# First expert step on idle accumulator banks, with its w1 sums on TensorE and the other sums of weights later

## The chip, the cores and the metric

The kernel runs on one core of one Trainium2 chip. The metric is the device time of one execution in microseconds. Of each kernel one execution was also profiled.

In the profile's lines PE is TensorE, PEld its weight loads, DVE is VectorE, ACT is ScalarE, POOL is GpSimd, SP is the queue that issues most loads. SBUF and PSUM are the memories on the chip; TensorE's results come into banks of PSUM. The granted clock is the share of TensorE's full clock that the trace gives: 1.00 (I call the array warm) or 0.50 (cold), with means between for a stretch that has both. A count such as "x4" counts records of the trace, and here one matmul leaves two of them.

## The reference, cut to what matters

```python
for c in range(nc):                        # Mamba-2 chunks, one after another
    cum = np.cumsum(np.log(a[chunk]))
    L = np.exp(cum_i - cum_j) * causal     # decays between positions
    y = ((C @ B.T) * L) @ x + (C @ state) * np.exp(cum)
    state = decay_full * state + sum(B x decay_from_j)
x = y.transpose(...)                       # 3072 tokens x 256
p = domain_probs / (domain_probs.sum(-1) + 1e-9)
for e in range(4):                         # four experts, 256 -> 1024 -> 256
    out += p[:, e] * (np.maximum(x @ w1[e], 0) @ w2[e])
```

The kernel handles a sequence in chunks of 128 positions and the experts in blocks of 512 tokens. There are six blocks of eight steps; a step is half of one expert. Each pair of matrix products in a step is done by a scheme of seven products in place of eight. The scheme needs sums of blocks of the weights (S1 to S4), sums of blocks of the tokens (yS) and sums of the seven results.

## The kernel before

The first block's four chunks have to pass before its first expert step can go beyond its first two products. These are the parts that matter. Names on the left of a `<-` in the profile are the tiles named here.

```python
def sums_of(op):                              # 4 GpSimd operations, then a store by GpSimd
    nc.gpsimd.tensor_add(op(S1), op(S3), op(A22))
    nc.gpsimd.tensor_sub(op(S2), op(S1), op(A11))
    nc.gpsimd.tensor_sub(op(S4), op(A12), op(S2))
    nc.gpsimd.tensor_sub(op(S3), op(A11), op(S3))

def decays(c):
    ...
    LT = att.tile([P, NH * P], FP32, tag="LT", name="LT", bufs=1)      # one buffer
    nc.vector.tensor_tensor_scan(out=LT, data0=s["ab"], data1=ident..., ...)
    ...
    nc.gpsimd.tensor_mul(bdec, xb..., s["LT"][:, :, P - 1:P]...)       # GpSimd reads LT
    ...
    nc.vector.tensor_tensor_scan(out=dec, data0=s["ah"], data1=zeros, ...)
    nc.gpsimd.tensor_mul(cts, s["ctm"], dec...)

for c in range(CPB):                          # the four chunks of the first block
    masks(c)                                  # ScalarE
    ...
    scores(c, acc_banks)                      # TensorE
    ...                                       # loads, gates (c == 0)
    if c == 2:
        opened(0)                             # products 1 and 2 of the first step
    decays(c)                                 # VectorE, GpSimd
    if c:
        carry(c - 1)                          # VectorE: S, M
    masked(c, range(NQ))                      # VectorE: MT
    added(c, ps_att, "att")                   # TensorE: A <- bdec
    outputs(c, ps_att, "att")                 # TensorE: y; ScalarE: yT
    if c == 1: load_chunk(4); sum_w1(0)       # GpSimd
    if c == 2: load_chunk(5); sum_w2(0)
total(0, 1, "11"); gated(0, "11", "z11"); sums(0); carry(CPB - 1)
sum_w1(1); sum_w2(1)

for n in range(NS + 1):                       # the steps, software-pipelined
    ...
    if c_in is not None:
        masks(c_in)
        decays(c_in)                          # a later chunk: LT, dec on VectorE
    ...
    smul(n - 1, 1); fmul(n, 6); snap(n, 6); smul(n - 1, 3)
    fmul(n, 5); fmul(n, 7); snap(n, 7)
    total(n, 7, "22")                         # VectorE: z from bank Y
    smul(n - 1, 7); smul(n - 1, 5)
    gated(n, "22", "z22")                     # VectorE: h
    ...
    fmul(n, 3)                                # into bank Y again: waits for that z
    ...
```

The order in each engine's queue is the program's order; the waits between engines are set by the tile framework.

## Time and profile before

| | before |
|---|---|
| median of the first three executions | 680.82 us (679.91 to 680.96) |
| the profiled execution | 678.77 us, span 677.0 us |
| TensorE busy | 643.3 us, 95% |
| VectorE busy | 504.7 us, 75% |
| GpSimd busy | 107.9 us, 75 of them before 120 us |

The shares of busy time hide two stages. From 53.5 us on TensorE works almost without a gap. Before that VectorE works through four chunks and one expert step, and TensorE mostly waits. The change is about that first stage alone. The page's slices of 17 us show it: in the rows below each character is a slice, and a digit the share of it that the engine was busy, in tenths.

```profile
PE   3779999999999999999999999999999999999995
PEld 1458788888888887888887888887888888888884
DVE  6979887697776867876878768668868776856655
```

### The profile page before, as it was taken

The numbers are of one execution on the slowest core, as the hardware profiler recorded it, in microseconds if no ns is written. First come the engines' busy times: TensorE is split into PE (matmuls) and PEld (weight loads), VectorE is DVE, ScalarE is ACT, GpSimd is POOL, SyncE is SP. The second block draws the span as 40 slices with busy tenths as digits, with TensorE's granted clock in tenths as the row PEclk, the third lists the DMA queues.
The fourth block names the chain that finished last, engine by engine and source line by source line (L and its number), as shares of the span: only waits on it lengthen the run. The fifth ranks groups of instructions, "written<-read, shape, count | busy, mean of one in ns | idle before, by whom it ended". The sixth has DMA issues, their size and how long they took to land.

```text
span 677.0 us, 9047 instructions
## 1 busy us (share of the span) xinstructions
PE 643.3 (95%) x3465; PEld 538.6 (80%) x3465; DVE 504.7 (75%) x821; ACT 116.2 (17%) x231; POOL 107.9 (16%) x153
## 2 busy tenths in 40 slices
PE   3779999999999999999999999999999999999995
PEld 1458788888888887888887888887888888888884
DVE  6979887697776867876878768668868776856655
ACT  1111112121211121121112111212211112111110
POOL 2976845001000002000002000002000000200000
PEclk9989999999999999999999999999999999999999
DMA  8997859636745554765364655554673543653202
GB/s 247 337 326 251 293 194 345 245 120 183 253 160 182 189 201 129 243 234 180 121 231 153 205 188 193 196 179 163 186 258 127 180 161 109 171 218 119 99 1 31
DMA packets 70938, 128.64 MB, mean 190 GB/s; under 512 B 29040, under 2 KB 52464, under 8 KB 70896
## 3 DMA queue, kind: packets, MB, share of 16 engines
q1 hardware_dynamic: 65688, 112.67, 49.3%
q0 software_dynamic: 2304, 14.68, 5.7%
q10 hardware_dynamic: 2904, 0.72, 0.5%
q8 instruction: 27, 0.44, 0.3%
q14 instruction: 15, 0.12, 0.1%
HBM read 109.99 MB, written 18.07 MB: 189 GB/s over the span
## 4 chain that ended last, share of the span: by engine, by line
PE 89%; DVE 6%; issue 0%; ACT 0%; POOL 0%; DMA 0%; DVEq 0%
PE acc L409 41%; PE X L365 24%; PE Y L365 19%; DVE h L387 2%; PE y L310 2%; PE g L271 2%; PE y L303 1%; DVE hT L394 1%; DVE LT L237 1%; DVE z L377 0%; DVE u L429 0%; PE A L292 0%; ACT snap L372 0%; DVE MT L281 0%; DVE ot L445 0%
## 5 line engine op out<-in xcount | busy, mean ns | idle before, releaser
L377 DVE TENSOR_TENSOR z<-Y,snap 128x512 f32<-128x512 f32 x144 | 99.0, 688 | 131.6 <-ACT snap L372 109.3
L409 PE MATMUL acc<-hT,wt 128*128 128x256 f32 x768 | 191.2, 382 | 0.0
L372 ACT COPY snap<-X 128x512 f32<-128x512 f32 x144 | 84.3, 585 | 487.8 <-PE X L365 481.5
L409 PEld LDWEIGHTS acc<-hT,wt 128*128 128x128 f32 x768 | 144.3, 190 | 25.4 <-issue 6.6
L409 PE MATMUL acc<-h,wt 128*128 128x256 f32 x576 | 148.3, 380 | 4.9 <-DVE u L429 4.9
L365 PE MATMUL X<-yS,wt 128*128 128x256 f32 x576 | 149.0, 381 | 0.7 <-ACT snap L372 0.7
L409 PEld LDWEIGHTS acc<-h,wt 128*128 128x128 f32 x576 | 108.9, 190 | 21.8 <-DVE u L429 7.3
L365 PEld LDWEIGHTS X<-yS,wt 128*128 128x128 f32 x576 | 110.4, 192 | 16.4 <-ACT snap L372 1.1
L387 DVE SCALAR_TENSOR_TENSOR h<-z,gate 128x512 f32<-128x512 f32 x144 | 104.5, 726 | 3.3
L365 PE MATMUL Y<-yT,wt 128*128 128x256 f32 x384 | 100.6, 385 | 1.5 <-DVE z L377 1.4
L365 PEld LDWEIGHTS Y<-yT,wt 128*128 128x128 f32 x384 | 72.7, 192 | 13.7 <-DVE z L377 2.3
L394 DVE TENSOR_TENSOR hT<-h,hT 128x512 f32<-128x512 f32 x96 | 69.7, 726 | 3.3
L394 DVE TENSOR_TENSOR hT<-h,h 128x512 f32<-128x512 f32 x96 | 66.8, 719 | 1.3
L244 POOL TENSOR_TENSOR bdec<-xb,LT 128x128 f32<-128x128 f32 x20 | 8.3, 413 | 343.8 <-issue 181.9
L237 DVE TENSOR_TENSOR_SCAN LT<-ab,ident 128x1024 f32<-128x1024 f32 x24 | 55.4, 2310 | 0.4
L365 PE MATMUL Y<-yS,wt 128*128 128x256 f32 x192 | 52.5, 397 | 2.1 <-DVE z L377 1.1
L365 PE MATMUL X<-yT,wt 128*128 128x256 f32 x192 | 50.6, 387 | 2.3 <-DVE MT L281 1.5
L365 PEld LDWEIGHTS X<-yT,wt 128*128 128x128 f32 x192 | 36.6, 193 | 9.1 <-DVE MT L281 2.3
L365 PEld LDWEIGHTS Y<-yS,wt 128*128 128x128 f32 x192 | 35.2, 192 | 8.9 <-DVE z L377 1.5
L281 DVE TENSOR_TENSOR MT<-g,LT 128x256 f32<-128x256 f32 x96 | 33.9, 414 | 10.5 <-PE g L271 10.4
L387 DVE SCALAR_TENSOR_TENSOR h<-X,gate 128x512 f32<-128x512 f32 x48 | 33.0, 688 | 6.1 <-PE X L365 6.1
L271 PE MATMUL g<-ctm,xb 32*128 32x256 f32 x192 | 19.0, 461 | 8.3 <-ACT ctm L262 8.3
(66 smaller groups left out, 267.1 us busy)
## 6 DMA issues: line engine op xcount, KB each, us to landing
wt<-w_d SPq DMA_DIRECT2D x80, 896.0 KB, 4.4
w_d<-wt POOLq DMA_DIRECT2D x16, 896.0 KB, 6.5
ab<-acut_d SPq DMA_DIRECT2D x22, 512.0 KB, 8.2
wt<-in_w_dram SPq DMA_DIRECT2D x32, 256.0 KB, 4.2
xb<-in_xbc_dram SPq DMA_DIRECT2D x24, 320.0 KB, 6.5
gate<-p_d SPq DMA_DIRECT2D x24, 256.0 KB, 6.0
out_dram<-ot SPq DMA_DIRECT2D x40, 64.0 KB, 2.0
ah<-ac_d SPq DMA_DIRECT2D x19, 64.0 KB
```

Source lines behind the costliest of these rows:

```text
L237: nc.vector.tensor_tensor_scan(out=LT, data0=s["ab"], data1=ident.rearrange("p h s -> p (h s)"), initial=0.0, op0=ALU.mult, op1=ALU.add)
L244: nc.gpsimd.tensor_mul(bdec, s["xb"][:, OB:OB + HN].rearrange("p (h n) -> p h n", h=NH), s["LT"][:, :, P - 1:P].to_broadcast([P, NH, N]))
L271: nc.tensor.matmul(out=g.rearrange("p t s -> p (t s)"), lhsT=s["xb"][k, OBT:OBT + P], rhs=s["ctm"][k].rearrange("p t s -> p (t s)"), start ...
L281: nc.vector.tensor_mul(s["MT"][:, h], s["g"][q], s["LT"][:, h])
L303: nc.tensor.matmul(out=y.rearrange("p t s -> p (t s)"), lhsT=state["M"].rearrange("p q d -> p (q d)"), rhs=s["cts"].rearrange("p t s -> p ...
L310: nc.tensor.matmul(out=y[32 * q:32 * q + 32, t], lhsT=xb[:, h * D:h * D + D], rhs=MT[:, NT * q + t], start=(first and t == 0), stop=True, ...
L365: nc.tensor.matmul(out=f[bank][:, j], lhsT=wt1[n][:, w, j * P:j * P + P], rhs=rhs, start=(i in (1, 2, 5) and j == 0), stop=(j == JJ - 1), ...
L372: nc.scalar.copy(out=s, in_=first[n]["X"])
L377: nc.vector.tensor_add(z, first[n]["Y"], first[n][i])
L387: nc.vector.scalar_tensor_tensor(out=h, in0=first[n][src], scalar=0.0, in1=g.unsqueeze(1).to_broadcast([P, JJ, HB]), op0=ALU.max, op1=ALU. ...
L394: nc.vector.tensor_sub(h[o], h[x], h[y])
L409: nc.tensor.matmul(out=acc[k, u][:, half], lhsT=w2_op(n, w)[:, j], rhs=rhs[:, j], start=(n % SPB == 0 and half == 0 and j == 0), stop=(n % ...
```

## The change

Its intent is to shorten the first stage. It does six things:

1. the decays are loaded ahead of the gates' input;
2. the gates are normalised on GpSimd (the reciprocal stays on VectorE) and stored a chunk later, and the loads of later weights follow them;
3. the w1 sums of the first step are made by TensorE, with the identity and the negative identity, in accumulator banks that are idle, and copied out by ScalarE;
4. all other sums of weights are made after the fourth chunk;
5. the first step has its own idle banks: X, Y and a third, Z, for which product 5 is done twice, so that one bank need not be read and added to in turn; the second step's first products are drawn forward;
6. masks are made one chunk earlier.

The core of the diff, with cuts marked:

```diff
+    def sum_w1_first():
+        ...
+        put(r1, ((1, S3), (1, A22)))                 # TensorE, lhsT = ident or minus
+        nc.scalar.copy(out=op(S1), in_=r1)
+        put(r2, ((1, A11), (-1, S3)))
+        put(r1, ((-1, A11),), first=False)
+        nc.scalar.copy(out=op(S3), in_=r2)
+        nc.scalar.copy(out=op(S2), in_=r1)
+        put(r2, ((1, A12), (-1, S2)))
+        nc.scalar.copy(out=op(S4), in_=r2)
+        nc.gpsimd.dma_start(out=w1_d[n], in_=wt1[n])
...
     for c in range(CPB):
-        masks(c)
+        scores(c, ((ps_s, "acc0"), (ps_s, "acc1"), (ps_f, "X"), (ps_f, "Y")))
...
+        if c == 1:
+            store_gates()
+            load_w2(0); load_w1(1); load_gate(0, 0); load_w2(1)      # four lines
+            sum_w1_first()
         if c == 2:
             opened(0)
         decays(c)
...
-        if c == 1:
-            load_chunk(4)
-            sum_w1(0)
-        if c == 2:
-            load_chunk(5)
-            sum_w2(0)
...
     sums(0)
+    sum_w1(1)
+    sum_w2(0)
+    sum_w2(1)
     carry(CPB - 1)
...
+    fmul(0, 5)
+    fmul(0, 6)
+    snap(0, 6)
+    fmul(0, 5, True)
+    fmul(0, 3, True)
+    total(0, 6, "12", "Z")
+    fmul(0, 7)
+    snap(0, 7)
+    ...
+    sum_w1(2)
+    sum_w2(2)
+    opened(1)
+    fmul(0, 4)
+    gated(0, "21", "X")
+    total(1, 1, "11")
+    gated(1, "11", "z11")
+    diff(0, "T3", "22", "12")          # and T1, T2, T4: the four differences hT
+    ...
-    for n in range(NS + 1):
+    for n in range(1, NS + 1):
```

More of the change, by code (lines that the diff above doesn't have):

```diff
@@ L159, in sum_w2, with put @@
             nc.gpsimd.dma_start(out=w2_d[n], in_=wt2[n])
+    acc_banks = [(ps_s, f"acc{q}") for q in range(NQ)]
+    def sum_w1_first():
+        n, (a_, b_) = 0, acc_banks[2:]
+        op = lambda w: wt1[n][:, w]
+        r1 = a_[0].tile([P, HB], FP32, tag=a_[1], name="r1")
+        r2 = b_[0].tile([P, HB], FP32, tag=b_[1], name="r2")
+        def put(r, terms, first=True):
+            for i, (sign, w) in enumerate(terms):
+                nc.tensor.matmul(out=r, lhsT=ident[:, 0] if sign > 0 else minus, rhs=op(w),
+                                 start=(first and i == 0), stop=True, skip_group_check=True)
+        put(r1, ((1, S3), (1, A22)))
[7 more added lines that the diff above has]
+        nc.gpsimd.dma_start(out=w1_d[n], in_=wt1[n])
     pr = const.tile([P, T // P, E], FP32, name="pr")
     a_sb = const.tile([NCH * NH // 2, 2, P], FP32, name="a_sb")
-    nc.scalar.dma_start(out=pr, in_=probs)
     nc.scalar.dma_start(
         out=a_sb, in_=a.rearrange("c h s -> (c h) s").rearrange("(p r) s -> p r s", r=2))
+    nc.scalar.dma_start(out=pr, in_=probs)
     load_tokens(0)
@@ L175 @@
         nc.gpsimd.tensor_copy(ident[:, h], ident[:, 0])
+    minus = const.tile([P, P], FP32, name="minus")
+    nc.gpsimd.tensor_scalar_mul(minus, ident[:, 0], -1.0)
     load_tokens(2)
@@ L194, in clip @@
         nc.vector.tensor_scalar(out=v, in0=v, scalar1=1e-6, scalar2=1.0, op0=ALU.max, op1=ALU.min)
-    total = const.tile([P, T // P, 1], FP32, name="total")
-    nc.vector.reduce_sum(total, pr, axis=mybir.AxisListType.X)
-    nc.vector.tensor_scalar_add(total, total, 1e-9)
-    nc.vector.reciprocal(total, total)
-    nc.vector.tensor_mul(pr, pr, total.to_broadcast([P, T // P, E]))
     clip(a_sb)
@@ L211, in store_decays @@
             out=ac_d.rearrange("c h s -> (c h) s").rearrange("(p r) s -> p r s", r=2), in_=a_sb)
+    ptot = const.tile([P, T // P, 2], FP32, name="ptot")
+    nc.gpsimd.tensor_add(ptot, pr[:, :, 0:2], pr[:, :, 2:4])
+    nc.gpsimd.tensor_add(ptot[:, :, 0:1], ptot[:, :, 0:1], ptot[:, :, 1:2])
+    nc.gpsimd.tensor_scalar_add(ptot[:, :, 0:1], ptot[:, :, 0:1], 1e-9)
     def store_gates():
+        nc.vector.reciprocal(ptot[:, :, 0:1], ptot[:, :, 0:1])
+        nc.gpsimd.tensor_mul(pr, pr, ptot[:, :, 0:1].to_broadcast([P, T // P, E]))
         rows = T // P * E
@@ L349, with fmul @@
     first, hid, acc = {}, {}, {}
-    def fmul(n, i):
+    def fmul(n, i, third=False):
         k = n // SPB
@@ L355, in fmul @@
         bank = "X" if i in (1, 6, 7, 4) else "Y"
-        if i in (1, 2, 5):
-            f[bank] = ps_f.tile([P, JJ, HB], FP32, tag=bank, name=bank)
+        if n == 0 and third:
+            bank = "Z"
+        begins = i in (1, 2, 5)
+        if begins:
+            pool, tag = (ps_f, bank) if n else (ps_s, {"X": "acc2", "Y": "acc3", "Z": "acc1"}[bank])
+            f[bank] = pool.tile([P, JJ, HB], FP32, tag=tag, name=bank)
         y, Y = yT[k], yS.get(k)
@@ L366, in fmul @@
                 out=f[bank][:, j], lhsT=wt1[n][:, w, j * P:j * P + P], rhs=rhs,
-                start=(i in (1, 2, 5) and j == 0), stop=(j == JJ - 1), skip_group_check=True)
+                start=(begins and j == 0), stop=(j == JJ - 1), skip_group_check=True)
     def snap(n, i):
@@ L372, in snap, with total @@
         nc.scalar.copy(out=s, in_=first[n]["X"])
-    def total(n, i, b):
+    def total(n, i, b, src="Y"):
         z = first[n]["z" + b] = ffn.tile([P, JJ, HB], FP32, tag="z", name="z", bufs=3)
-        nc.vector.tensor_add(z, first[n]["Y"], first[n][i])
+        nc.vector.tensor_add(z, first[n][src], first[n][i])
     def gated(n, b, src):
@@ L460 @@
     nc.scalar.mul(warm, tmask[:, 0:1], tmask[:, 0:1])
-    acc_banks = [(ps_s, f"acc{q}") for q in range(NQ)]
+    masks(0)
+    store_decays()
     for c in range(CPB):
-        masks(c)
+        scores(c, ((ps_s, "acc0"), (ps_s, "acc1"), (ps_f, "X"), (ps_f, "Y")))
         if c == 0:
-            store_decays()
-        scores(c, acc_banks)
-        if c == 0:
+            load_decays(2, nc.sync)
+            load_chunk(3)
+        if c == 1:
             store_gates()
-            load_decays(2, nc.sync)
             load_w2(0)
+            load_w1(1)
             load_gate(0, 0)
-            load_chunk(3)
-            load_w1(1)
             load_w2(1)
+            sum_w1_first()
         if c == 2:
@@ L480 @@
         masked(c, range(NQ))
+        if c + 1 < CPB:
+            masks(c + 1)
         added(c, ps_att, "att")
         outputs(c, ps_att, "att")
-        if c == 1:
-            load_chunk(4)
-            sum_w1(0)
-        if c == 2:
-            load_chunk(5)
-            sum_w2(0)
+        if c in (1, 2):
+            load_chunk(c + 3)
     total(0, 1, "11")
@@ L491 @@
     sums(0)
+    sum_w1(1)
+    sum_w2(0)
+    sum_w2(1)
     carry(CPB - 1)
-    sum_w1(1)
-    sum_w2(1)
+    fmul(0, 5)
[6 more added lines that the diff above has]
+    snap(0, 7)
+    gated(0, "12", "z12")
+    total(0, 7, "22")
+    gated(0, "22", "z22")
+    load_gate(0, 1)
+    load_w1(2)
+    load_w2(2)
+    sum_w1(2)
[6 more added lines that the diff above has]
+    diff(0, "T3", "22", "12")
+    diff(0, "T1", "12", "11")
+    diff(0, "T2", "22", "T1")
+    diff(0, "T4", "21", "T2")
     both = nc.sync, nc.sync
-    for n in range(NS + 1):
+    for n in range(1, NS + 1):
         k, r = divmod(n, SPB)
@@ L513 @@
                 load_w2(n + 2)
-            if n:
+            if n > 1:
                 opened(n)
@@ L527 @@
         if run:
-            if n == 0:
-                fmul(n, 5)
             fmul(n, 6)
@@ L538 @@
         if run:
-            if n:
-                fmul(n, 5)
+            fmul(n, 5)
             fmul(n, 7)
```

## The prediction

> **What bounds the kernel now.** I read the page's slices first, then the stages, then each engine's timeline of the start. The stages (columns: stretch, its length, then each engine's busy us with its instructions, granted clock, DMA share, GB/s) show where there is anything to win:
>
> ```profile
> 0.00:6.50 6.50, 1.37 (x9) 0.67 (x9) 1.84 (x16) 2.16 (x4) 2.40 (x13) 1.00 0.72 207
> 6.50:33.00 26.50, 15.20 (x135) 8.36 (x134) 24.84 (x45) 4.10 (x12) 16.71 (x20) 0.99 0.92 312
> 33.00:53.50 20.50, 16.31 (x56) 12.30 (x56) 16.44 (x22) 3.52 (x7) 14.69 (x20) 0.84 0.92 329
> 53.50:120.00 66.50, 64.96 (x362) 54.03 (x363) 56.26 (x77) 11.08 (x23) 41.13 (x53) 1.00 0.78 271
> 120.00:640.00 520.00, 515.73 (x2771) 437.75 (x2770) 385.85 (x631) 90.68 (x177) 32.97 (x49) 1.00 0.53 180
> ```
>
> From 53.5 to 640 us TensorE is busy 580.7 of 586.5 us. The change leaves those steps alone, so it can only move the moment at which they begin. Before 53.5 us TensorE is busy 32.9 us and idle 20.6 us, but from 6.5 to 33 us VectorE is busy 24.84 of 26.5: four attention chunks run one after another on VectorE, some 6 us each. Its timeline says where it does wait:
>
> ```profile
> 18.27 2.29 DVE L237 TENSOR_TENSOR_SCAN LT<-ab,ident 128x1024 f32<-128x1024 f32 x1
> ...
> 23.95 2.92 DVE L237 TENSOR_TENSOR_SCAN LT<-ab,ident 128x1024 f32<-128x1024 f32 x1
> ...
> 32.69 0.42 DVE L343 TENSOR_TENSOR yS<-yT 128x256 f32<-128x256 f32 x1 [0.56 <-ACT yT L317]
> ...
> 39.01 0.69 DVE L377 TENSOR_TENSOR z<-Y,snap 128x512 f32<-128x512 f32 x1 [1.84 <-ACT snap L372]
> ...
> 41.86 0.69 DVE L377 TENSOR_TENSOR z<-Y,snap 128x512 f32<-128x512 f32 x1 [1.17 <-PE Y L365]
> 43.29 0.69 DVE L387 SCALAR_TENSOR_TENSOR h<-X,gate 128x512 f32<-128x512 f32 x1 [0.73 <-PE X L365]
> ...
> 52.83 0.67 DVE L377 TENSOR_TENSOR z<-Y,snap 128x512 f32<-128x512 f32 x1
> ```
>
> The brackets are idle time and what ended it. Between 7 and 53 us VectorE waits 0.56 + 1.84 + 1.17 + 0.73 = 4.3 us, nearly all in the first expert step, where one bank Y is added up, read, added to again and read again. The rest is work, so the start is a VectorE chain with a few holes. The hand-over to the steady state is TensorE's block at 53.55, freed by that last z:
>
> ```profile
> 53.55 1.13 PE L365 MATMUL Y<-yT,wt 128*128 128x256 f32 x4
> ```
>
> **What the Trainium skill says.** *SBUF — State Buffer*, "Who interferes with whom": VectorE and GpSimd share a port pair as an exclusive lock; a VectorE instruction with two SBUF inputs contends with a GpSimd one that reads SBUF, while one with a single SBUF input does not. The trace agrees:
>
> ```profile
> 17.51 0.73 POOL L146 TENSOR_TENSOR wt<-wt 128x256 f32<-128x256 f32 x1
> 18.32 2.76 POOL L147 TENSOR_TENSOR wt<-wt 128x256 f32<-128x256 f32 x1
> ```
>
> A sum of weights takes 0.73 us alone and 2.76 under the scan LT that began at 18.27. In the other direction LT took 2.92 instead of 2.29 at 23.95.
>
> *PSUM — Partial Sum Buffer*, "Engine vs sequencer instructions": the GpSimd queue is a strict FIFO. The trace agrees: bdec of the fourth chunk could have run at 26.87, when its LT ended, but stood behind the sums and their store:
>
> ```profile
> 29.18 0.59 POOL L159 DMA_DIRECT2D w_d<-wt  x1 [0.31 <-DVE M L335]
> 29.79 0.42 POOL L244 TENSOR_TENSOR bdec<-xb,LT 128x128 f32<-128x128 f32 x1
> ```
>
> *TensorE: Matmul & The Clock Gate*, Part 1: after an idle window of about 3.4 us the array runs at half rate. The trace has it: four matmuls take 2.07 us at 33.17 and 39.75, and 1.13 at 53.55; the granted clock of that stretch is 0.84.
>
> **The change part by part.**
>
> 1. *Decays first.* Before, a_sb was issued at 1.19, landed at 6.5, and VectorE waited 1.49 us for it. It now goes 0.45 us earlier. The first ab, issued at 1.20 behind the same traffic, lands at about the same time, and its clip now starts at 7.18. Estimate: −0.4 us.
>
> 2. *Gates on GpSimd.* The four VectorE operations on the gates lay at 3.94 to 5.04, in VectorE's wait for a_sb, so removing them gives nothing. The reciprocal (0.30 us) moves into the VectorE chain of the second chunk: +0.3 us.
>
> 3. *Sums of w1 for the first step by TensorE.* Removed from GpSimd: 0.77 + 0.73 + 2.76 + 0.84 = 5.1 us; added: seven 256-column matmuls, cold at about 0.5 us each (2.07/4), so 3.5 us, and four ScalarE copies of 0.37 us in alternation. They follow the second chunk's scores (about 14 us) and the gates' transpose. With the hand-overs the last copy ends near 18.5. The trap is that the store of these weights stands on the GpSimd queue ahead of the second chunk's bdec, which ran at 15.14. Now it runs after about 19.2, then meets LT of the third chunk (18.3 to 20.5) and gets the port at about 20.5. cts follows to about 22, outputs of chunk 2 to about 24, the third chunk's scores about 24.5, where VectorE needed them at 22.46. Estimate: +1.7 us, the part that I trust least.
>
> 4. *Other sums later.* Set against the same shapes from 120 to 600 us, VectorE's slowed operations between 6.5 and 53.5 us cost about 7 us: h 5 × 0.25, dec 4 × 0.30, M 4 × 0.18, S 3 × 0.31, the four differences 1.3, LT 0.7, the yS sums 0.9. That comes with 24 GpSimd sums; 20 stay and overlap about the same kind of work, now all after the fourth bdec. So the slowing falls by about a sixth: −1.2 us. Also bdec and cts of chunk 4 no longer stand behind sums, which is what makes VectorE's 0.56 us wait for yT.
>
> 5. *Idle banks, product 5 twice.* Four matmuls more (0.9 us warm). z for 12 and for 22 come from separate banks, so TensorE no longer waits for VectorE's read of Y (1.40 us) and for h (0.78). VectorE's 4.3 us of holes go, but the chain product 6, copy, product 7, copy, z stays, and more matmuls precede the first z. If TensorE is cold when it starts there, five blocks of four at up to 2 us reach z later than VectorE is free. Estimate: 4.3 us removed, 1.5 us of new holes.
>
> 6. *Masks a chunk earlier.* This takes 1.05 us from TensorE before each of three scores. VectorE was never waiting for these, so nothing by itself; it softens part 3.
>
> Sum: −0.4 + 0.3 + 1.7 − 1.2 − 4.3 + 1.5 = −2.4 us at that block of Y. From there to the end the kernel is TensorE-bound and the shift should be kept, except that GpSimd's five remaining sums (4.4 us each) now end near 51 instead of 48.66, inside a second step that starts earlier: its h and differences are slowed longer. I take back 0.4 for that. Net −2.0; the slack in part 3 (masks earlier, warm array) is worth perhaps 1 us, so I settle on −2.8 us: 680.8 − 2.8 = 678.0 us.
>
> **The rivals.**
>
> *VectorE simply loses its holes.* No new wait in chunk 2, array warm from chunk 2 on: 4.3 + 1.2 + 0.1, up to 6 us: about 675. For it: VectorE was continuously busy up to 31 us with TensorE's waits hidden. Against: the FIFO on GpSimd.
>
> *The store in front of bdec becomes the wait.* If identity sums, copies and store end past 21 us, chunks 2 to 4 shift by 3 us or more, and only the holes pay it back: 680 to 682. For it: cold matmuls and three round trips between TensorE and ScalarE.
>
> *GpSimd becomes the bound.* The second step needs S2 of its w1 and S4 of the first w2. Sums starting near 29 us finish two tiles at about 38, before TensorE wants them (about 41). Only if weights land late does it bite: 680 or more. Against: weights are issued before 20 us and the DMA share of 0.92 is no higher than before.
>
> **Range and chances.** Everything at stake lies in 47 us, and VectorE's own work there is over 40, so 13.6 us (2%) cannot be won; losing it would take a wait no view suggests. The central case is 678.0, 8 in 10 from 674.5 to 681.0. Faster by over 2%: 0.01; within: 0.98; slower: 0.01.
>
> **What would show it right or wrong.** (a) VectorE's first clip of ab about 0.4 us earlier. (b) bdec of the second chunk at 19 us or later, straight after the store of w_d, and VectorE idle before MT of the third chunk; if bdec still runs near 15 to 17, part 3 is wrong and the gain nearer 5. (c) LT of chunk 4 back at 2.29, dec near 0.62, bdec of chunk 4 just after LT. (d) the four listed VectorE holes gone or under 2 us together. (e) the second step's first block into Y from yT 2 to 4 us before 53.55, and the stretch from there to the end as long as before, within 1 us. If that stretch shrinks or grows by more, the shift is not simply carried along and my account is wrong.

## The result, and the profile after

| | before | changed |
|---|---|---|
| median of four executions, same rounds | 680.52 us | 680.57 us |
| range | 679.91 to 680.96 | 679.54 to 681.89 |
| ratio | | 1.0002, 95% interval 0.9982 to 1.0022 |

A ratio is the mean time of one kernel's runs over that of the other's in the same rounds, so it isn't quite the ratio of the medians. The time lies inside the range on record, but the gain of 2.8 us that was its centre isn't there.

The changed kernel's timeline of VectorE answers the lines that the prediction quotes (start in us, duration, engine, line, operation, tiles; in brackets the idle time before it and what ended it):

```profile
6.74 0.69 DVE L220 TENSOR_SCALAR ab<-ab 128x1024 f32<-128x1024 f32 x1 [2.12 <-DMA ab<-in_a_dram]
...
16.07 1.41 DVE L309 TENSOR_TENSOR MT<-g,LT 128x256 f32<-128x256 f32 x4
19.38 2.80 DVE L265 TENSOR_TENSOR_SCAN LT<-ab,ident 128x1024 f32<-128x1024 f32 x1 [1.90 <-POOL bdec L272]
...
25.49 2.29 DVE L265 TENSOR_TENSOR_SCAN LT<-ab,ident 128x1024 f32<-128x1024 f32 x1
...
32.73 1.23 DVE L371 TENSOR_TENSOR yS<-yT 128x256 f32<-128x256 f32 x1 [0.19 <-ACT yT L345]
...
39.63 0.69 DVE L409 TENSOR_TENSOR z<-Z,snap 128x512 f32<-128x512 f32 x1 [0.77 <-PE Z L397]
...
43.01 0.69 DVE L419 SCALAR_TENSOR_TENSOR h<-X,gate 128x512 f32<-128x512 f32 x1 [0.56 <-PE X L397]
...
50.06 2.28 DVE L265 TENSOR_TENSOR_SCAN LT<-ab,ident 128x1024 f32<-128x1024 f32 x1
...
52.57 0.66 DVE L409 TENSOR_TENSOR z<-Y,snap 128x512 f32<-128x512 f32 x1
```

The four holes of before (0.56, 1.84, 1.17 and 0.73 us) have become 0.19, 0.77 and 0.56, as intended. But a new one of 1.90 us stands before LT of the third chunk, the first of the sums yS takes 1.23 us where it took 0.42, and the z that ends the list comes at 52.57: only 0.26 us before its place in the kernel before (52.83).

TensorE, in its own timeline, is ahead by far more than that and then waits for this z:

```profile
47.13 1.93 PE L441 MATMUL acc<-hT,wt 128*128 128x256 f32 x8
53.29 2.08 PE L397 MATMUL Y<-yT,wt 128*128 128x256 f32 x4 [4.23 <-DVE z L409]
55.16 1.91 PE L397 MATMUL X<-yS,wt 128*128 128x256 f32 x4
```

In the kernel before, the same block started at 53.55 without waiting and took 1.13 us. Here it takes 2.08. The stretch from 52.5 to 56 us, first in the kernel before, then in the changed one (stretch, its length, busy us of PE, PEld, DVE, ACT and POOL, granted clock, DMA share, GB/s):

```profile
52.50:56.00 3.50, 3.40 (x16) 2.68 (x15) 2.97 (x6) 0.00 (x0) 3.09 (x5) 1.00 0.16 64
```

```profile
52.50:56.00 3.50, 2.71 (x6) 2.19 (x7) 2.19 (x4) 0.00 (x0) 3.34 (x5) 0.50 0.38 159
```

The clock is at half. From the block into Y to the third step's first product it is 60.94 − 53.29 = 7.65 us, against 58.81 − 53.55 = 5.26 before. So the changed kernel, 0.26 us ahead at the hand-over, is 2.13 us behind at the third step. It wins 1.4 us of that back: before, TensorE lost 1.3 us between 70 and 80 us (busy 8.70 of 10), and the changed kernel loses 0.2 there (9.81). From there to the end it is late by a constant 0.74 us. I call that number the **lag** of a kernel: the start of its eighth LT minus that of the kernel before (117.9 us), negative where the kernel is ahead. After this point it stays the same to within 0.03 us in every kernel.

One caution on lags: they compare two profiled executions. That of the kernel before took 678.77 us, 0.9 to 1.8 us less than its medians here (679.66 to 680.52), so that lags make other kernels look worse by about this much. Those of the others lie between 1.5 us below their median (banks_only) and 3.3 us above it (no_sums). Part of this spread goes with the clock, which no run here controls: of the 31 executions of the kernel before in the later rounds, the nine with a mean granted clock of 0.99 or more took 678.5 to 679.5 us, and the sixteen at 0.985 or less took 679.6 to 681.5. Its profiled execution had 0.993.

The slowing of VectorE is seen in groups by form, up to this z: line, engine, operation, tiles, forms, count, then busy us and the mean ns of one, then idle time before. First before:

```profile
L387 DVE SCALAR_TENSOR_TENSOR h<-z,gate 128x512 f32<-128x512 f32 x4 | 3.9, 964 | 0.1
L252 DVE TENSOR_TENSOR_SCAN dec<-ah,zeros 128x128 f32<-128x128 f32 x4 | 2.8, 693 | 0.0
L394 DVE TENSOR_TENSOR hT<-h,h 128x512 f32<-128x512 f32 x2 | 2.2, 1154 | 0.0
...
L327 DVE SCALAR_TENSOR_TENSOR S<-S,dec 128x32 f32<-128x32 f32 x3 | 1.7, 560 | 0.1
```

Then the changed kernel:

```profile
L419 DVE SCALAR_TENSOR_TENSOR h<-z,gate 128x512 f32<-128x512 f32 x4 | 2.9, 720 | 0.1
L426 DVE TENSOR_TENSOR hT<-h,h 128x512 f32<-128x512 f32 x2 | 2.9, 1467 | 0.0
L355 DVE SCALAR_TENSOR_TENSOR S<-S,dec 128x32 f32<-128x32 f32 x3 | 2.8, 924 | 0.1
...
L280 DVE TENSOR_TENSOR_SCAN dec<-ah,zeros 128x128 f32<-128x128 f32 x4 | 1.6, 403 | 0.0
```

dec and h got their normal lengths back (about 400 and 690 ns), but hT and S lost more than that. I sum up, over LT, dec, M, S, h, yS and hT from 6.5 us to this z, how much longer each took than its mean between 120 and 600 us (2285, 398, 292, 252, 692, 417 and 690 ns). This **excess** is 6.8 us before, with 24 GpSimd sums in that stretch, and 7.8 us in the changed kernel, with 20.

### The profile page after: what moved, and what is told of

Same layout as the page of the kernel before. It is cut to its first block, busy times and chain, and to the rows that moved or that the text cites. A ratio compares the mean times of both kernels' runs of the same rounds, so it can differ in the third digit from the quotient of the medians. Undisturbed runs are those within 1.5% of the kernel's fastest.

```text
span 677.7 us, 9087 instructions
## 1 busy us (share of the span) xinstructions
PE 645.9 (95%) x3483; PEld 541.8 (80%) x3483; DVE 500.9 (74%) x818; ACT 118.0 (17%) x235; POOL 104.8 (15%) x154
## 3 DMA queue, kind: packets, MB, share of 16 engines
HBM read 109.99 MB, written 18.07 MB: 189 GB/s over the span
## 4 chain that ended last, share of the span: by engine, by line
PE 90%; DVE 5%; issue 0%; ACT 0%; DVEq 0%
PE acc L441 41%; PE X L397 24%; PE Y L397 19%; PE y L338 2%; DVE h L419 2%; PE g L299 2%; PE y L331 1%; DVE hT L426 1%; DVE LT L265 1%; DVE z L409 0%; DVE u L461 0%; PE A L320 0%; PE Z L397 0%; DVE MT L309 0%; DVE ot L477 0%
## 5 line engine op out<-in xcount | busy, mean ns | idle before, releaser
L441 PEld LDWEIGHTS acc<-hT,wt 128*128 128x128 f32 x768 | 144.8, 191 | 25.8 <-issue 6.6
L419 DVE SCALAR_TENSOR_TENSOR h<-z,gate 128x512 f32<-128x512 f32 x144 | 101.9, 708 | 3.3
L397 PE MATMUL Y<-yT,wt 128*128 128x256 f32 x380 | 98.6, 382 | 4.2 <-DVE z L409 4.2
L397 PEld LDWEIGHTS Y<-yT,wt 128*128 128x128 f32 x380 | 71.3, 191 | 15.8 <-DVE z L409 4.6
L426 DVE TENSOR_TENSOR hT<-h,hT 128x512 f32<-128x512 f32 x96 | 68.0, 709 | 3.3
L283 POOL TENSOR_TENSOR cts<-ctm,dec 128x256 f32<-128x256 f32 x20 | 14.5, 726 | 75.4 <-DVE dec L280 75.4
```

Source lines behind the costliest of these rows:

```text
L283: nc.gpsimd.tensor_mul(cts, s["ctm"], dec.unsqueeze(1).to_broadcast([HN, NT, P]))
L397: nc.tensor.matmul(out=f[bank][:, j], lhsT=wt1[n][:, w, j * P:j * P + P], rhs=rhs, start=(begins and j == 0), stop=(j == JJ - 1), skip_gro ...
L419: nc.vector.scalar_tensor_tensor(out=h, in0=first[n][src], scalar=0.0, in1=g.unsqueeze(1).to_broadcast([P, JJ, HB]), op0=ALU.max, op1=ALU. ...
L426: nc.vector.tensor_sub(h[o], h[x], h[y])
L441: nc.tensor.matmul(out=acc[k, u][:, half], lhsT=w2_op(n, w)[:, j], rhs=rhs[:, j], start=(n % SPB == 0 and half == 0 and j == 0), stop=(n % ...
```

## The experiments

My theory after the traces was this. The holes were removed, worth 2.8 us, and two things ate that before the hand-over: the store of w1 in front of the second chunk's bdec (1.9 us), and more slowing by the port that VectorE and GpSimd share, rather than less (+1.0 in place of −1.2). After the hand-over a cold array costs more. The main rival was that VectorE's total work sets the pace up to the fourth step, so that nothing moved within it shows at the end. The twelve kernels below are all that ran. Each is an edit of the changed kernel unless it says otherwise. All gave the right result, apart from the two that are wrong on purpose.

| kernel | median us (kernel before in the same rounds) | ratio, 95% interval | z of the second step | lag |
|---|---|---|---|---|
| changed | 680.57 (680.52) | 1.0002, 0.9982 to 1.0022 | 52.57 | +0.74 |
| store_later | 677.94 (679.66) | 0.9990, 0.9976 to 1.0003 | 51.19 | −1.33 |
| z_first | 677.67 (679.66) | 0.9979, 0.9966 to 0.9992 | 51.55 | −0.17 |
| warm | 683.49 (679.66) | 1.0060, 1.0047 to 1.0072 | 52.65 | +4.39 |
| no_sums (wrong result) | 674.95 (679.66) | 0.9937, 0.9909 to 0.9964 | 52.25 | −0.56 |
| both | 675.29 (680.01) | 0.9934, 0.9922 to 0.9947 | 48.19 | −3.52 |
| warm9 | 680.82 (680.01) | 1.0017, 1.0001 to 1.0034 | 54.33 | +1.96 |
| lt_two | 679.60 (680.01) | 0.9991, 0.9976 to 1.0007 | 52.04 | +0.77 |
| banks_only | 679.06 (680.01) | 0.9987, 0.9972 to 1.0003 | 51.15 | −1.17 |
| banks_z | 676.75 (680.24) | 0.9949, 0.9935 to 0.9963 | 49.37 | −2.35 |
| undo3 | 677.65 (680.24) | 0.9963, 0.9946 to 0.9980 | 50.77 | −1.15 |
| before_no_sums (wrong result) | 672.32 (680.24) | 0.9883, 0.9864 to 0.9902 | 47.80 | −5.02 |
| best | 674.95 (680.24) | 0.9918, 0.9902 to 0.9934 | 48.31 | −3.41 |

### store_later: the store of w1 behind the second chunk

```diff
 def sum_w1_first():
     ...
-    nc.gpsimd.dma_start(out=w1_d[n], in_=wt1[n])
...
         outputs(c, ps_att, "att")
+        if c == 1:
+            nc.gpsimd.dma_start(out=w1_d[0], in_=wt1[0])
```

> The changed kernel with one edit: the store of the first step's w1 leaves its place on the GpSimd queue ahead of the second chunk's bdec and comes after that chunk's outputs. Theory A (FIFO on GpSimd): bdec of chunk 2 runs at about 15, right after its LT, instead of 18.91, VectorE's idle 1.90 us before LT of chunk 3 is gone, LT starts at about 17.4, and all of VectorE's chain up to the z of the second step (52.57) comes 1.5 to 2 us earlier; the end too: about 678.7. Rival B (VectorE merely meets more GpSimd work or a wait for a load later): LT of chunk 3 starts earlier but the z stays within 0.5 us of 52.57 and the time at 680.5. Rival C: ab of chunk 3 has not landed, so the idle time stays and its releaser becomes a DMA.

GpSimd's timeline, first the changed kernel's, then this one's:

```profile
18.10 0.79 POOL L183 DMA_DIRECT2D w_d<-wt  x1 [5.59 <-ACT wt L182]
18.91 0.43 POOL L272 TENSOR_TENSOR bdec<-xb,LT 128x128 f32<-128x128 f32 x1
```

```profile
14.95 0.41 POOL L271 TENSOR_TENSOR bdec<-xb,LT 128x128 f32<-128x128 f32 x1 [2.40 <-DVE LT L264]
15.79 0.72 POOL L282 TENSOR_TENSOR cts<-ctm,dec 128x256 f32<-128x256 f32 x1 [0.42 <-DVE S L352]
18.22 0.79 POOL L517 DMA_DIRECT2D w_d<-wt  x1 [1.72 <-DMA ah<-ac_d]
```

bdec runs right after its LT, 4 us earlier, and LT of the third chunk starts at 18.07 with no idle time before it (I had said 17.4: dec and M are slowed again, now that bdec and cts run beside them). The z comes 1.38 us earlier and the lag falls by 2.1 us, to −1.33. Theory A holds in the trace: a single DMA start at a bad place on a strict FIFO queue cost up to 1.9 us. The ratio alone, 0.9990, doesn't settle it: three of its five runs lie at 677.6 to 677.9, two at 679.4 and 679.9.

### z_first: LT of the fifth chunk behind z and h

```diff
 for n in range(1, NS + 1):
     ...
-    if c_in is not None:
-        masks(c_in)
-        decays(c_in)
-    if n + 2 < NS: sum_w1(n + 2); sum_w2(n + 2)
+    if n > 1: enter_chunk()            # the same lines, as a function
     ...
         gated(n, "22", "z22")
+    if n == 1: enter_chunk()
```

> The changed kernel with one edit: in the second step LT and dec of chunk 4 (2.3 + 0.4 us on VectorE) come after z and h of product 7 and not before. Theory A (TensorE idles 4.23 us for that z because VectorE does LT first, then runs cold for 6.8 us): the block into Y starts at about 50.6 instead of 53.29, TensorE's wait is about 1.5 us, the array stays warm, and the third step's first block comes 2 to 4 us before 60.94; the end 1 to 2 us earlier, about 679, as LT then stands in the way of the next z. Rival B (VectorE's total is what counts, its order not): the block comes earlier but the third step's first blocks come at 60.5 to 61.5 all the same, time 680.5.

```profile
52.29 1.13 PE L397 MATMUL Y<-yT,wt 128*128 128x256 f32 x4 [1.74 <-DVE z L409]
...
59.16 1.13 PE L397 MATMUL X<-yT,wt 128*128 128x256 f32 x4 [0.69 <-DVE MT L309]
```

TensorE waits 1.74 us in place of 4.23, and the next block takes 1.13 us, so the array is warm. (The masks, bdec, cts and sums of weights that stand behind LT in the program move with it; in the changed kernel the first of these sums starts at 53.55, after the z, so they don't explain its earlier start.) In this execution the hole in chunk 2 was longer (2.51 us) and the start 0.5 us later, so that the fourth LT was 2.60 us behind the kernel before, against 1.53 in the changed kernel. Nevertheless the block into Y came at 52.29, not at 53.29, and the lag is −0.17, not +0.74. The ratio, 0.9979, excludes 1. The block didn't come at 50.6 as I had said, and the third step began 1.78 us before 60.94, not 2 to 4; the longer hole and the later start explain 1.07 us of these misses. The order has a price, as expected: LT, and with it MT, now come later, and from the block into Y to the end z_first, both, banks_z and best each lose 1.1 us against the kernel before. Rival B (order doesn't matter, only VectorE's total) falls.

### warm and warm9: filling TensorE's wait

```diff
     smul(n - 1, 5)
+    if n == 1:
+        fill = ps_att.tile([P, HB], FP32, tag="att", name="fill")
+        for i in range(20):            # 9 in warm9
+            nc.tensor.matmul(out=fill, lhsT=ident[:, 0], rhs=wt1[0][:, 0], start=True, stop=True)
```

> The changed kernel with twenty matmuls more, on an idle bank, in TensorE's 4.23 us of idle time before the block into Y. Theory A (the cold array costs 2.4 us there, of which 1.35 is won back by the fourth step): the block starts at 53.3 to 53.5 but takes 1.1 instead of 2.08 us, the third step begins about 2.2 us earlier, and from 75 us on the lag against the kernel before is -0.3 instead of +0.74: about 679.5. Rival B (VectorE sets the pace of steps two to four): blocks are faster but the lag from 75 us on stays at +0.7, time 680.5.

This was a mis-sized experiment, and its expectation missed. The trace has 40 records for 20 matmuls:

```profile
48.96 8.80 PE L603 MATMUL fill<-wt,ident 128*128 128x256 f32 x40
57.60 1.03 PE L397 MATMUL Y<-yT,wt 128*128 128x256 f32 x4
```

I had read an "x4" of a product as four matmuls, where it is two matmuls of two records each (the next expectation calls these records passes). The fill overran the hole by 4.3 us and the kernel lost 4.05 us at the hand-over; its lag of +4.39 shows that such a loss is passed on whole to the end.

> The fill of the kernel warm again, now nine matmuls and not twenty (each was two passes of 0.216 us, so twenty took 8.8 us and overshot the hole by 4.3): 3.9 us in a hole of 4.23. Theory A (the cold array costs about 2.4 us after the hand-over): the block into Y starts at 53.2 to 53.5 and takes 1.1 us, the third step's first block comes 1.8 to 2.4 us before 60.94, and the lag from 75 us on is about -0.3 in place of +0.74, time 1 us less than the changed kernel's. Rival B (VectorE sets the pace): the lag from 75 us on stays within 0.3 us of +0.74.

With nine matmuls the fill fits. The clock in the stretch from 52.5 to 56 us is full again:

```profile
52.50:56.00 3.50, 3.28 (x15) 2.58 (x14) 3.36 (x4) 0.00 (x0) 1.09 (x2) 1.00 0.62 262
```

From the block into Y (55.04) to the third step (60.30) it is 5.26 us, exactly as in the kernel before; the cold array thus costs 7.65 − 5.26 = 2.39 us at that place, as I had said. But the time is no better (680.82, ratio 1.0017), and the lag is +1.96. The profiled execution says why its lag can't be compared directly: its hole in chunk 2 was 3.05 us, since the identity products ran on a cold array themselves (the first six records took 2.52 us, against 1.46 in the changed kernel), and the block into Y was 1.49 us behind the kernel before. What can be compared is what is added between this block and the end: 1.96 − 1.49 = 0.47 us. The kernels whose clock is at 0.50 all through that stretch add 1.0 (changed), 1.6 (lt_two) and 0.9 (undo3); those where it is higher (warm and warm9 1.00, store_later 0.65, banks_only 0.57) add 0.3 to 0.5. So of 2.4 us lost on the spot some 0.4 to 1.3 us remain at the end, by the traces of single executions; the times didn't resolve it, and the expectation of a lag of −0.3 missed.

### no_sums and before_no_sums: what the shared port costs

The sums of weights of the first step are replaced by fills with zeros, which read nothing. The results are wrong. before_no_sums is the same edit in the kernel before.

```diff
-def sums_of(op):
+def sums_of(op, skip=False):                 # called with skip = n < 3
+    if skip:
+        for w in (S1, S2, S4, S3):
+            nc.gpsimd.memset(op(w), 0.0)
+        return
```

> The changed kernel with the twenty GpSimd sums of the first step (w1 of steps 1 and 2, w2 of 0, 1 and 2) replaced by fills with zeros, which read nothing; the result is wrong on purpose. Theory A (the lock on the shared port, more of it than before, ate the gain): the four yS differences after 32.7 take 0.42 us each and not 0.83 to 1.23, the four differences hT 0.7 each and not 1.1 to 1.4; the z of the second step comes 4 to 5 us before 52.57; the end 3 to 5 us earlier, 676 to 677. Rival B (TensorE's chain of products is as late): VectorE's operations get shorter but waits for z and h take their place, and the z comes less than 2 us earlier.

> The kernel before with its twenty-four GpSimd sums of the first step replaced by fills with zeros that read nothing; the result is wrong on purpose. It measures my estimate of 7 us of slowing on VectorE by the shared port. Theory A: the excess over the durations of 120 to 600 us falls from 6.8 us to under 1.7 us (in the changed kernel without sums it was 1.6), but waits for TensorE take part of it, so the z of the second step comes 3 to 5 us before 52.83; 675 to 677.5. Rival B (other things slow VectorE at the start, such as transfers): the excess stays above 3 us.

The excess falls from 7.8 to 1.6 us in the changed kernel and from 6.8 to 1.0 in the kernel before. The four yS sums take 0.42 us each. In before_no_sums the groups shown above read:

```profile
L391 DVE SCALAR_TENSOR_TENSOR h<-z,gate 128x512 f32<-128x512 f32 x4 | 2.8, 688 | 0.1
L256 DVE TENSOR_TENSOR_SCAN dec<-ah,zeros 128x128 f32<-128x128 f32 x4 | 1.8, 452 | 0.0
...
L398 DVE TENSOR_TENSOR hT<-h,h 128x512 f32<-128x512 f32 x2 | 1.3, 688 | 0.0
```

So the slowing comes from the GpSimd sums, which read SBUF, as the Trainium skill has it (SBUF — State Buffer, "Who interferes with whom"). The fills are also shorter (four in 1.07 us, where one sum takes 0.73), and no run separates the reading from the length. The kernel before without the sums is 1.2% faster (672.32 against 680.24), the largest gain of any edit here. Its z comes 5.03 us earlier, at the edge of what was expected, and the time even beat the expectation. That kernel's array also stays warm from about 27 us on, so not all of its gain is the port's.

no_sums missed at the z, which came at 52.25, not 4 to 5 us earlier; its median, 674.95 us, is below the 676 to 677 expected. Its profiled execution was the slowest of four (678.22; the others 672.5 to 675.8), with a start 1 us later and a hole of 3.01 us in chunk 2; by then it was 3.59 us behind the kernel before, and a hole of 4.53 us before the first z of 12 (with TensorE cold again) took part of what the shorter operations gave. Rival B, that TensorE's chain takes the place of VectorE's, is half true here. The two medians say one thing more: without sums the changed kernel (ratio 0.9937, 0.9909 to 0.9964) is slower than the kernel before without sums (0.9883, 0.9864 to 0.9902), with four runs of each. So the changed kernel loses something that isn't the port's.

### lt_two: two buffers for LT

```diff
-LT = att.tile([P, NH * P], FP32, tag="LT", name="LT", bufs=1)
+LT = att.tile([P, NH * P], FP32, tag="LT", name="LT", bufs=2)
```

> The changed kernel with two buffers for LT in place of one; the store stays ahead of bdec. Theory A (VectorE's idle 1.90 us is a wait for LT's only buffer, which the late bdec still reads): LT of chunk 3 starts at about 17.5 without idle time. Then the lock: bdec of chunk 2 (ready at 18.9) runs only after that LT, at about 20, the third chunk's scores come at about 22.5, and MT of chunk 3 starts at 23 to 24 against 23.99, so that under 1 us of the 1.9 is won. Rival B (the idle time is a wait for something else, ab's landing above all): LT starts at 19 or later all the same.

LT of the third chunk starts at 17.39 without idle time: the hole was indeed a wait for LT's only buffer, which the late bdec still read. And the loss comes back one station later, for the scores:

```profile
17.39 2.28 DVE L265 TENSOR_TENSOR_SCAN LT<-ab,ident 128x1024 f32<-128x1024 f32 x1
...
23.71 1.42 DVE L309 TENSOR_TENSOR MT<-g,LT 128x256 f32<-128x256 f32 x4 [1.83 <-PE g L299]
```

MT starts at 23.71 in place of 23.99 us. This is the route that the prediction had described: late bdec, late cts, late outputs, late scores. A second buffer only moved the wait; the lag stays at +0.77.

### both: the two edits together

> The changed kernel with both edits: the store of w1 after the second chunk's outputs, and LT of chunk 4 after z and h of product 7 in the second step. Theory A (two separate losses on one chain: up to 1.9 us of FIFO and buffer wait in chunk 2, then the order and the cold array at the hand-over): they add; LT of chunk 3 at about 18 without idle, the block into Y at about 49.5 to 50.5, the lag against the kernel before -2.5 to -3.5 us from 75 us on; ratio about 0.996. Rival B (a later wait in steps two to four takes whatever comes earlier): the lag stays at -1.3 as with the store moved alone, ratio 0.998 to 0.999.

```profile
48.92 1.13 PE L396 MATMUL Y<-yT,wt 128*128 128x256 f32 x4 [1.73 <-DVE z L408]
```

Theory A: they add, and more. LT of the third chunk at 18.09, block into Y at 48.92 with a wait of 1.73 us, array warm, lag −3.52, 675.29 us against 680.01 (ratio 0.9934). Against the changed kernel the lag falls by 4.26 us, where the two edits alone brought 2.07 and 0.91; z_first's longer hole and later start, 1.07 us, are most of the rest. Its runs lie between 675.17 and 675.95, a narrow range. That fits with the store no longer passing on to VectorE how cold TensorE was in the identity products, but isn't shown.

### banks_only and banks_z: part 5 alone on the kernel before

banks_only is the kernel before with the new first step (the lines from the first `fmul(0, 5)` to the last `diff` of the diff above, with their banks) and nothing else of the change. banks_z adds the order edit of z_first.

> The kernel before with part 5 alone: the first step on idle banks, product 5 twice, the second step's first products drawn forward; sums, gates, decays and masks as in the kernel before. Theory A (VectorE's holes of 4.3 us fall to about 1.5, the rest of the change brings the loss): the z of the second step 2 to 3 us before 52.83, and since the array turns cold while it waits, about 1.5 us of it left from 75 us on: lag -1 to -2. Rival B (part 5 too is worth nothing, because GpSimd's sums slow VectorE as much as the holes did): z within 1 us of 52.83, lag within 0.7 us of 0.

The z comes 1.68 us earlier, somewhat less than the 2 to 3 expected, as the four hT take 4.98 us in place of 4.05: all four now run beside GpSimd sums (which end at 48.2 us), where before the last one came after them. TensorE waits 4.23 us for the z here too. The lag is −1.17, the ratio 0.9987. So part 5 alone is better than the whole change, in the traces; the times don't separate them.

> The kernel before with two things alone: part 5 (idle banks, product 5 twice) and the order edit of z_first (LT of chunk 4 after z and h of product 7). Sums, gates, decays, masks as before. Theory A (part 5 and the order are what pays, the other parts of the change are worth under 1 us together once the store is out of the way): block into Y at 48.5 to 50, array warm, lag -2.5 to -3.5 us, ratio 0.994 to 0.996, within 1 us of the kernel both. Rival B (parts 1 to 4 and 6 carry a good part of the gain of both): lag -1.2 to -2, ratio 0.997 to 0.998.

The lag is −2.35 and the ratio 0.9949: part 5 and the order of two VectorE groups bring two thirds of the lag of both and 0.51 of its 0.66%. The rest of the change is worth about 1.2 us of lag (−3.52 against −2.35) once the store is out of the way; I had said under 1. The lag also falls just short of the −2.5 to −3.5 that Theory A gave.

### undo3: the first w1 sums back on GpSimd

```diff
-            sum_w1_first()
...
         if c in (1, 2):
             load_chunk(c + 3)
+        if c == 1:
+            sum_w1(0)
```

> The changed kernel with part 3 undone: the first step's w1 sums on GpSimd again, at the end of chunk 2, as in the kernel before; all else as changed. Theory A (part 3 costs the wait of 1.9 us in chunk 2 and saves only little slowing): no idle time before LT of chunk 3, which starts at 17.4 to 18.1; LT of chunk 3 or 4 slowed; the z of the second step 1 to 1.8 us before 52.57 and the lag -0.5 to -1.5 in place of +0.74, much as with the store moved (-1.33). Rival B (sums on TensorE pay for themselves): the z no earlier than 52.3, lag +0.5 or more.

LT of the third chunk starts at 18.07 without a hole, the z comes 1.80 us earlier, lag −1.15: as Theory A has it, and within 0.2 us of store_later. Only the slowing of LT did not come (2.29 and 2.31 us). Sums on TensorE, well placed, are worth no more than sums on GpSimd between chunk 2 and chunk 3; by the times they may be worth less, with a ratio of 0.9990 (0.9976 to 1.0003) for store_later against 0.9963 (0.9946 to 0.9980) here, intervals that barely overlap. They cost 14 records, seven matmuls (13.89 to 17.38 us in the changed kernel), and four ScalarE copies and save four GpSimd operations that, there, run beside MT and LT.

### best: each step sums w2 of the next step

both, and with it:

```diff
     sums(0)
     sum_w1(1)
     sum_w2(0)
-    sum_w2(1)
...
     sum_w1(2)
-    sum_w2(2)
+    sum_w2(1)
...
                 sum_w1(n + 2)
-                sum_w2(n + 2)
+                sum_w2(n + 1)
```

> The kernel both with one thing more: each step sums w2 of the next step and not of the one after, so that four sums of weights and not five fall into the first step. Theory A (the rest of the slowing is in proportion to the sums that overlap VectorE's chain): up to the z 16 GpSimd sums in place of 20, excess 0.5 to 1.5 us less than the 7.9 of both, lag -3.8 to -5 against -3.52; about 674.5. Rival B (the sums only move, and slow steps two to four instead): lag -3.2 to -3.7, the time that of both, 675.3.

The excess falls from 7.9 to 6.3 us as expected, but the first z from Z waits 2.11 us in place of 0.64: VectorE comes to it 0.7 us sooner, while TensorE's product comes 0.75 us later (0.5 us of that is a later start of this execution). The lag is −3.41, where both has −3.52. The median is 674.95 us, the lowest of the correct kernels, with a ratio of 0.9918 (0.9902 to 0.9934) against 0.9934 (0.9922 to 0.9947) of both. The intervals overlap: that best beats both is not shown. Both beat the kernel before and the changed one clearly.

## Why the prediction was right or wrong

The range held, but only by 0.4 us at its upper end, and the centre was 2.6 us off. That a change worth nothing still lay inside is owed to the width of the range, 6.5 us, and not to the sum. Its own sum, against what the profiles show at the z of the second step:

| part | predicted | measured | from |
|---|---|---|---|
| 1, decays first | −0.4 | −0.44 | first clip of ab, 7.18 to 6.74 |
| 2, reciprocal into the chain | +0.3 | +0.29 | its duration at 11.44 |
| 3, store ahead of bdec | +1.7 | +1.90 | hole before LT of chunk 3 |
| 4, slowing by the shared port | −1.2 | +1.0 | excess, 6.8 to 7.8 |
| 5, holes of the first step | −4.3 + 1.5 | −4.30 + 1.52 | 0.19 + 0.77 + 0.56 left |
| sum at the hand-over | −2.4 | −0.03; the z itself: −0.26 | 52.83 to 52.57 |
| from there to the end | +0.4 − 0.8 | +1.0 | −0.26 at the hand-over, lag +0.74 |

The sum leaves 0.23 us at the z unexplained. Of the prediction's own five signs (a), (c) and (d) came, dec even at 0.40 us. Of (b) the store and the late bdec came (18.10 and 18.91), but not the place of the wait. Sign (e) failed: the block into Y came 0.26 us earlier, not 2 to 4, and the stretch from there to the end grew by 1.0 us. The second rival had named 680 to 682 for the time, but by another road: the store ran at 18.10, not past 21, and the fourth LT came 1.53 us late, not 3.

**Right.** That only the start can move, since TensorE bounds the rest: 515.73 us busy from 120 to 640 us in both kernels, and a constant lag. That VectorE's chain decides the start. Parts 1, 2 and 5, the last to a few hundredths of a microsecond, which is partly luck. And the mechanism of part 3, a store at the head of a FIFO queue: store_later and undo3 each take the loss away.

**Right in size, wrong in place.** I had overlooked, in part 3, that LT has one buffer. I expected idle time before MT of chunk 3 for late scores; it came before LT. lt_two shows that the route I described is what comes next when the buffer is doubled. The 3.5 us for the seven identity products was right by two errors that cancelled: a matmul here is two records, not one, and the array was warm for most of them. For the same reason the "four matmuls" of 2.07 us are two. They ran at half rate, but the trace does not show an idle window of 3.4 us before them: between 24 and 40 us TensorE's longest idle time was 1.54 us. What it does show stands in the last section. (Nor is the clock of 0.99 for 6.50:33.00 to be trusted: the product X at 21.51 took 2.07 us too, and the trace's clock record begins only at 25.8.)

**The step that failed first: part 4.** I took the slowing to be in proportion to the number of sums, "the slowing falls by about a sixth". It rose, although four sums were gone. In the chunks a part of VectorE's work was not slowed: MT and z take one input from PSUM and kept 0.41 to 0.43 and 0.66 to 0.69 us. The change moved the sums under yS, S and hT, which have two SBUF inputs: S rose from 0.9 to 2.0 us of excess, yS from 0.9 to 2.3, hT from 1.3 to 2.4, while dec and h lost 2.1 together. What counts, beside their number, is which operations the sums meet. (Where the placement is kept, the number does count: best has four sums fewer than both, 16 against 20, and 6.3 us of excess against 7.9, which is in proportion.) That the sums are the cause is shown by no_sums and before_no_sums; that this pairing is the reason for the rise is my reading of which groups rose. Nor does the rise alone make the change worth nothing: banks_only has an excess as large (8.0 us) and a lag of −1.17.

**The step that failed second: "the shift should be kept".** I made the hand-over one point in time, and took off 0.4 us for slower h and differences. But TensorE ended its last products before this z at 49.06, where before it was 53.45, so that the queue order on VectorE (four differences, LT, dec and only then z) became the bound: 4.23 us of idle time in which the array went cold. I had looked at this place for a wait and seen none, because in the kernel before TensorE came too late to show it. z_first cuts the wait to 1.74 us and keeps the array warm; banks_only (4.23 us) and banks_z (0.83 us) show the same on the kernel before. The cold array's 2.39 us is shown by warm9 on the spot; that some 0.4 to 1.3 us of it reaches the end rests on lags of single executions.

**Left open.** How much of the changed kernel's spread (679.5 to 681.9) comes from the hole in chunk 2, which was 1.90 to 3.05 us in the profiles of the five kernels with the store in place and one LT buffer. It follows the identity products: their first six records took 1.46, 1.55, 1.98, 2.47 and 2.52 us, and the hole was 1.90, 2.08, 2.51, 3.01 and 3.05 us, each time 0.4 to 0.5 us more. So it grew with the time that these products spent on a cold array, but no run fixed the array's state there.

## What to carry to other kernels

When you take a wait away from one engine, look at what the engine that it waited for does next in program order, and at the clock of the array that will now idle there: here moving two VectorE operations behind the one awaited, and one DMA start behind the operation that others need, turned a change worth nothing into one worth 0.7%. A queue's store is not free of charge for what stands behind it, and a second buffer only moved that wait here. If GpSimd works beside VectorE, ask which VectorE operations it meets, and not only how many operations it has.

## What the Trainium skill lacked or had wrong

- SBUF — State Buffer, "Who interferes with whom": the rule held, but the page has no size for a chain of operations. Here VectorE's operations with two SBUF inputs took 0.83 to 1.47 us for 0.42 to 0.69 beside GpSimd sums, and all that slowing came to 6.8 us in the first 53 us; with fills, which only write, 1.0 us is left.
- The same page's list of which operations contend has no scan, though its rule on two SBUF inputs covers one. The scan LT (128x1024) blocked a GpSimd sum for 2.76 us in place of 0.73, and took 2.80 to 2.92 in place of 2.29 where it ran beside GpSimd work.
- TensorE: Matmul & The Clock Gate, Part 1: its half rate comes after at least one idle window of about 3.4 us. In the kernel before, the clock fell to 0.50 at 32.6 and again at 39.4 us, though TensorE had been busy for 1.59 of the 3.40 us before the first fall and 1.68 of the 3.40 us before the second. So a window that is about half busy was followed by half rate too. Nor did equal idle time give equal cold time: after the same wait of 4.23 us the block into Y took 2.08 us in the changed kernel and 1.13 in banks_only, whose next block was the one slowed. The page's remark that its window runs freely fits with that.
- FP8 and Floating Point Precision, "TensorE Precision Notes" has true fp32 as four passes; no page that I found says that the trace holds two records for one matmul. Twenty matmuls of 256 columns gave 40 records and took 8.80 us, 0.44 us each.
